# Half of w1's columns in blocks of 128, 128, 96 and 96 rows

## The chip, the core and the metric

The kernel runs on one core of one Trainium2 chip. The core has five engines with instruction streams of their own: PE (matrix multiplication), DVE (vector), ACT (activations), POOL and SP. 16 DMA engines move data between HBM and the on-chip memory; here only SP issues transfers. The metric is the device time of one execution in microseconds (us). Before the change the median of three runs is 676.2 us (675.98 to 676.47).

## The reference

A decode step for two rows of x (2 x 448): attention over a cache of 16 heads x 4096 positions x 256, and beside it a small two-layer network with a ReLU; a gate mixes the two. All in float32.

```python
q = (x @ wq).reshape(B, Sq, 16, 256).transpose(0, 2, 1, 3)
scores = jnp.einsum("bhqd,bhkd->bhqk", q, k_cache) * (256 ** -0.5)
o = jnp.einsum("bhqk,bhkd->bhqd", softmax(scores), v_cache)
a = o.transpose(0, 2, 1, 3).reshape(B, Sq, 4096) @ wo
b = jnp.maximum(x @ w1, 0) @ w2          # w1: 448 x 1792, w2: 1792 x 448
g = sigmoid((x * gate_w).sum(-1, keepdims=True))
return g * a + (1 - g) * b
```

## The kernel before

**Data.** Nearly all bytes are the cache: 32 units (2 rows x 16 heads), each 128 partitions x 64 KB, half K and half V (`kv`). The on-chip memory holds a ring of three slots of 64 KB per partition. Everything that is large goes through these slots: first `wq` and `xg` (slot 0), then the units in turn, at the end `w1` and `w2` (slot 0, as two parts of the array `wm`) and `wo` (slot 1). xg, the last columns of wq's rows, holds x and the gate's weights in chunks of the contraction.

**Order of the transfers.** SP issues all of them, so they form one queue, and each of the 16 DMA engines works off its own share in this order. SP waits until a slot is free (the semaphore `freed`, counted by DVE after each unit) and then issues the next load into it, so that one to two loads are always queued behind the running one. After the last unit come `w1` (L170), `w2` (L171) and, when unit 30 is done, six parts of `wo` (L175): 14, 8, 4, 3, 2 and 1 blocks of 448 columns, each with a semaphore of its own.

**The main loop.** For each unit PE multiplies q with K into `sc` (L131), DVE takes the maximum (L351), ACT the exponential (L318), and DVE multiplies V with it and sums, in eight instructions (L356). ACT keeps the result (L323).

**w1.** D = 448 is 3 x 128 + 64 (`KF` = 3 full chunks, `KC` = 4 chunks). The 1792 columns are four groups of 448 (`G` = 4, `FG` = 448); group g accumulates in the partitions 32 g to 32 g + 31 of `pa`. `project` (L108) does the full chunks with one matmul per chunk and group (L111). The last 64 rows of two groups are stacked in 128 partitions, and a stationary operand `xl` with zeros in the right places does both groups in one matmul of 64 columns (L114). So each half of w1's columns (two groups) has 6 x 448 + 448 columns in 128 partitions, and w1 has `W1` = 6272 columns in all. ACT makes `xr` (x repeated for the full chunks, L297), `xn` (L298) and `xl` (L301) from xg at the start.

**The tail on PE.** `pe_tail` waits for w1 (`w1_in`) and does chunks 0 and 1 (`hidden(0, 2)`), waits until all units are done (`freed` = 32), transposes the maxima `nm` and the sums `ls` of the partial softmaxes (L234, L235), does chunk 2, multiplies the weights `wb` of the parts (L238), and does the last chunk (`hidden(KF, KC)`). ACT then applies the ReLU (L327), PE transposes the result (L250, L252), ACT repeats it (L329, L332), and 14 matmuls with w2 follow (L258). DVE in the meantime scales the attention output and spreads it (`oc`, L372). Then wo: 26 blocks in `acc` as they land (L270), one copy (L375), a fold (L278), the last 6 blocks directly (L283), and the result goes out (L377, L178). A float32 matmul shows as two MATMUL records.

Of the kernel before, what the change touches and what calls it, by code (L numbers as in the profile page):

```python
# [4 lines left out]
AF = mybir.ActivationFunctionType  # L5
# [4 lines left out]
P, HP = 128, 64  # L10
G = 4
R = P // G
# [3 lines left out]
DIRECT = (3, 2, 1)  # L16


def gated_mix_decode(nc, wq, kv, wm, wo, out):
    U, _, SW = kv.shape  # L20
    D = 448
    B = 2
    RB = R // B
# [4 lines left out]
    KC, KF = 4, 3  # L28
    H = U // B
    HH = H // G  # L30
    NW = wq.shape[1] - KC * (B + 1)
    FG = 448
    NF = 14
    W1 = 2 * (2 * KF * FG + FG)
    DG = D // G
    NO = HH * J
    SCALE = float(DH) ** -0.5
    pe, dve, act, pool, sp = nc.tensor, nc.vector, nc.scalar, nc.gpsimd, nc.sync
# [12 lines left out]
    slot = [ring[:, i * SW:(i + 1) * SW] for i in range(SLOTS)]  # L51

    def sb(name, *shape):
        t = nc.alloc_sbuf_tensor(name, list(shape), F32)
        assert nc.sbuf_base <= first
        return t.ap()
# [6 lines left out]
    last_v, w1_in, w2_in = ev(), ev(), ev()  # L63
# [11 lines left out]
    xr = sb("xr", P, KF, P // B, B)  # L75
    xl = sb("xl", P, 2, RB, B)
    xn = sb("xn", P, P // B, B)
    ge = sb("ge", P, 1)
    gp = sb("gp", P, 1)
    omg = sb("omg", P, 1)  # L80
# [7 lines left out]
    p = sb("p", P, SG)  # L88
# [10 lines left out]
    pa = ps("pa", P, CW)  # L99
# [5 lines left out]
    def x_of(c, n=R):  # L105
        return xr[:, c].rearrange("p r b -> p (r b)")[:, :n]

    def project(dst, w, at, at_last, n, lo, hi):  # L108
        for c in range(lo, min(hi, KF)):
            for g in range(G):  # L110
                m = pe.matmul(dst[g * R:(g + 1) * R, :n], x_of(c), w[:, at(c, g):at(c, g) + n], start=(c == 0), stop=False)  # L111
        if hi == KC:
            for i in range(2):
                m = pe.matmul(dst[i * HP:(i + 1) * HP, :n], xl.rearrange("p j r b -> p (j r b)"),  # L114
                              w[:, at_last(i):at_last(i) + n], start=False, stop=True)
        return m

    xg = slot[0][:, NW:wq.shape[1]].rearrange("p (c b) -> p c b", c=KC)

    ident_0, ident_ok, par_ok, fold_ok, xl_0 = (ev() for _ in range(5))  # L120
    x_ok, gate_mm, gate_ok, ge_ok, gp_ok, omg_ok = (ev() for _ in range(6))
# [23 lines left out]
    ml_tr, nb_ok, e_ok, el_ok, rl_ok, wb_ok, wp_mm, os_ok, po_mm, oc_ok = (ev() for _ in range(10))  # L145
    acc_mm, a_ok, z_mm, res_ok = ev(), ev(), ev(), ev()
    w1 = slot[0][:, :W1]
    w2 = slot[0][:, W1:W1 + NF * D]
    w_o = slot[1]

    with nc.Block(no_gpsimd_drain=True) as block:

        @block.sync
        def _(_e):
            sp.wait_ge(q_mm, 2)
            sp.dma_start(slot[0], kv[2]).then_inc(slot_in[0], 16)
            with nc.Fori(0, LOOP - 2, engines=(ET.SP,)) as r:
                u0 = sp.snap(r * SLOTS)
                for k in range(SLOTS):
                    s = (k + 1) % SLOTS  # L160
                    sp.wait_ge(freed, u0 + k + 1)
                    sp.dma_start(slot[s], kv[bass.ds(u0 + k + SLOTS, 1)].rearrange("o p n -> (o p) n")  # L162
                                 ).then_inc(slot_in[s], 16)
            sp.wait_ge(freed, U - 4)
            sp.dma_start(slot[1], kv[U - 2]).then_inc(slot_in[1], 16)
            sp.wait_ge(freed, U - 3)
            sp.dma_start(slot[2][:, :SW // 2], kv[U - 1][:, :SW // 2]).then_inc(slot_in[2], 16)
            sp.dma_start(slot[2][:, SW // 2:], kv[U - 1][:, SW // 2:]).then_inc(last_v, 16)
            sp.wait_ge(freed, U - 2)
            sp.dma_start(w1, wm[:, :W1]).then_inc(w1_in, 16)  # L170
            sp.dma_start(w2, wm[:, W1:]).then_inc(w2_in, 16)  # L171
            sp.wait_ge(freed, U - 1)
            k = 0
            for n, s in zip(ACC + DIRECT, wo_in):
                sp.dma_start(w_o[:, k * D:(k + n) * D], wo[:, k * D:(k + n) * D]).then_inc(s, 16)  # L175
                k += n
            sp.wait_ge(res_ok, 1)
            sp.dma_start(out, res[0:7 * 15 + 1:7, :]).then_inc(out_sem, 16)  # L178
# [13 lines left out]
        def pe_main():  # L192
# [7 lines left out]
            for i in range(2):  # L200
                if i:
                    pe.wait_ge(q_ok, i)
                project(pb, slot[0][:, i * NW // 2:(i + 1) * NW // 2], lambda c, g: g * W + c * CW,
                        lambda i: G * W + i * CW, CW, 0, KC).then_inc(q_mm, 1)
# [18 lines left out]
                pe.end_ifs()  # L223

        def pe_tail():
            half = W1 // 2
            def hidden(lo, hi):
                return project(pa, w1, lambda c, g: g // 2 * half + (g % 2 * KF + c) * FG,
                               lambda i: i * half + 2 * KF * FG, FG, lo, hi)

            pe.wait_ge(w1_in, 16)
            hidden(0, 2)
            pe.wait_ge(freed, U)
            pe.transpose(pc[:U, :P], nm, ident)  # L234
            pe.transpose(pc[:U, P:2 * P], ls, ident).then_inc(ml_tr, 1)  # L235
            hidden(2, KF)
            pe.wait_ge(wb_ok, 1)
            pe.matmul(pb[:, :U], wb.rearrange("u g r -> u (g r)"), ident[:U, :U], start=True,  # L238
                      stop=True).then_inc(wp_mm, 1)
            hidden(KF, KC).then_inc(hid_mm, 1)  # L240
            pe.wait_ge(fold_ok, 1)
            pe.wait_ge(os_ok, 1)
            n = HH * B * J
            for g in range(G):
                m = pe.matmul(pc[g * R:(g + 1) * R, :n], sel,
                              os.rearrange("p u j -> p (u j)")[:, g * n:(g + 1) * n], start=True, stop=True)
            m.then_inc(po_mm, 1)
            pe.wait_ge(hid_ok, 1)
            for t in range(KF):
                pe.transpose(pb[:, t * P:(t + 1) * P], hs[:, t * P:(t + 1) * P], ident)  # L250
            for j in range(2):
                m = pe.matmul(pb[j * HP:(j + 1) * HP, KF * P:], hs[:, KF * P:], ident, start=True, stop=True)  # L252
            m.then_inc(hid_tr, 1)
            pe.wait_ge(w2_in, 16)
            pe.wait_ge(hr_ok, 1)
            for k in range(NF):
                g = k % G
                pe.matmul(acc[g * R:(g + 1) * R, :D], hr[:, k, :], w2[:, k * D:(k + 1) * D], start=(k < G),  # L258
                          stop=False)

            def o_of(k):
                return oc[:, k // J, k % J].rearrange("p r b -> p (r b)")

            pe.wait_ge(oc_ok, 1)
            k, n = 0, sum(ACC)
            for i, a in enumerate(ACC):
                pe.wait_ge(wo_in[i], 16)
                for _ in range(a):
                    g = k % G
                    m = pe.matmul(acc[g * R:(g + 1) * R, :D], o_of(k), w_o[:, k * D:(k + 1) * D], start=False,  # L270
                                  stop=(k >= n - G))
                    k += 1
            m.then_inc(acc_mm, 1)
            for i, a in enumerate(DIRECT):
                if i == 0:
                    pe.wait_ge(a_ok, 1)
                    for g in range(G):
                        pe.matmul(z[g * R:(g + 1) * R, :DG], fold.rearrange("p r b -> p (r b)"),  # L278
                                  a_sb[:, g * DG:(g + 1) * DG], start=(i == 0), stop=False)
                pe.wait_ge(wo_in[len(ACC) + i], 16)  # L280
                for _ in range(a):
                    for g in range(G):
                        m = pe.matmul(z[g * R:(g + 1) * R, :DG], o_of(k),  # L283
                                      w_o[:, k * D + g * DG:k * D + (g + 1) * DG], start=False,
                                      stop=(k == NO - 1))
                    k += 1
            m.then_inc(z_mm, 1)
# [7 lines left out]
        def _(_e):  # L295
            act.wait_ge(slot_in[0], 16)
            act.activation(xr, xg[:, :KF, None, :B].to_broadcast([P, KF, P // B, B]), AF.Copy)  # L297
            act.activation(xn, xg[:, KF:, :B].to_broadcast([P, P // B, B]), AF.Copy)  # L298
            act.wait_ge(xl_0, 1)
            for j in range(2):  # L300
                a = act.activation(xl[j * HP:(j + 1) * HP, j], xg[j * HP:(j + 1) * HP, KF:, :B]  # L301
                                   .to_broadcast([HP, RB, B]), AF.Copy)
            a.then_inc(x_ok, 1)
            act.wait_ge(gate_mm, 1)
# [1 line left out]
            for i in range(2):  # L306
# [3 lines left out]
                a = act.activation(qt[:, i * U // 2:(i + 1) * U // 2, :].rearrange("p (s n) t -> p s t n", s=2),  # L310
                                   pc.rearrange("p (s t x) -> p s t x", s=2, t=T)[:, :, :, ::17], AF.Copy)
# [18 lines left out]
            for j in range(2):  # L330
                r = slice(j * HP, (j + 1) * HP)
                a = act.activation(hr[r, KF * G:, :],  # L332
                                   pb[r, KF * P + j * HP:KF * P + (j + 1) * HP].rearrange("p (k r) -> p k r", r=R),
                                   AF.Copy)
# [103 lines left out]
```

## Time and profile before

| | us |
|---|---|
| median of 3 runs | 676.2 |
| the profiled execution | 676.38 |
| its span, first to last instruction | 674.8 |
| PE busy | 213.0 |
| DVE busy | 339.8 |
| ACT busy | 54.2 |

The profiled execution's own time is 1.6 us longer than its span; this is what lies before the first and after the last recorded instruction. A row of the timeline gives the start, the duration, the engine, the line and what the instruction writes and reads; in brackets stands the idle time before it and what ended it. A row of the table of windows gives for each engine the busy time and the number of instructions in that stretch, and then PE's granted clock, the mean busy share of the 16 DMA engines, and their rate. A row of the queue table gives the packets that started in the asked window, their megabytes, and the time that they took as a share of 16 engines over that window. Queue q1 holds the transfers that SP issues, q8 the loading of instructions.

### The profile page before, as it was taken

The page shows a single profiled execution, that of the slowest core. Times are in us where ns is not written, and L with a number is a line of the kernel's source. Part 1 is how long each engine was busy: PE and PEld are TensorE (multiplying, and loading weights), DVE is VectorE, ACT ScalarE, POOL GpSimd, SP SyncE. Part 2 cuts the span into 40 slices and gives each one's busy share as a digit, 9 for nine tenths or more (in the row PEclk, how much of TensorE's full clock was granted, in tenths as well). Part 3 has the DMA queues.
Part 4 walks back from the last instruction along what each step waited for, and adds up shares of the span by engine and source line. Part 5 has one row for each costly group of instructions (what it writes and reads, how often), then busy time and mean ns, then how long its engine had stood idle before and what let it go on. Part 6 is the DMA issues. An engine that isn't in the chain of part 4 may idle for free.

```text
span 674.8 us, 4173 instructions
## 1 busy us (share of the span) xinstructions
PE 213.0 (32%) x1279; PEld 52.0 (8%) x1279; DVE 339.8 (50%) x561; ACT 54.2 (8%) x144; POOL 1.1 (0%) x9
## 2 busy tenths in 40 slices
PE   0633221333332123333321233333222333332455
PEld 0210000000000000000000000000000000000011
DVE  0024566545455665544656654455566445456670
ACT  0110000000000000000000000000000000000110
POOL 0000000000000000000000000000000000000000
PEclk9976567767655676776656677665667767655879
DMA  9999999999999999999999999999999999999997
GB/s 381 427 435 436 435 435 435 435 435 435 435 435 435 435 435 435 435 435 435 431 435 435 435 435 435 435 435 435 435 435 435 435 435 435 435 435 406 420 437 304
DMA packets 6082, 289.59 MB, mean 429 GB/s; under 512 B 704, under 2 KB 832, under 8 KB 1216
## 3 DMA queue, kind: packets, MB, share of 16 engines
q1 hardware_dynamic: 6080, 289.55, 99.3%
q8 instruction: 2, 0.03, 0.0%
HBM read 289.54 MB, written 0.01 MB: 429 GB/s over the span
## 4 chain that ended last, share of the span: by engine, by line
DMA 70%; DVE 12%; PE 9%; issue 6%; DVEq 1%; ACT 1%; SPq 0%; ACTq 0%
DMA ring<-in_kv 65%; DVE ring L356 10%; PE sc L131 9%; DMA ring<-in_wo 4%; DVE nm L351 2%; DVEq L356 1%; ACT p L318 1%; PE z L283 0%; DVEq L348 0%; DVEq L353 0%; PE acc L270 0%; SPq L175 0%; SPq L162 0%; DVEq L351 0%; DVE a_sb L375 0%
## 5 line engine op out<-in xcount | busy, mean ns | idle before, releaser
L356 DVE SCALAR_TENSOR_TENSOR ring<-ring,p 128x1024 f32 x256 | 295.9, 1222 | 54.8 <-ACT p L318 54.8
L131 PE MATMUL sc<-ring,qc 128*32 128x512 f32 x1024 | 182.6, 878 | 417.8 <-DMA ring<-in_kv 417.8
L351 DVE TENSOR_REDUCE nm<-sc 128x1024 f32 x32 | 39.2, 1225 | 236.1 <-PE sc L131 236.1
L131 PEld LDWEIGHTS sc<-ring,qc 128*32 128x32 f32 x1024 | 41.2, 154 | 558.6 <-issue 558.6
L318 ACT ACTIVATE p<-sc,nm 128x1024 f32<-128x1024 f32 x32 | 35.7, 1114 | 257.8 <-DVE nm L351 257.8
L323 ACT ACTIVATE ov<-on 128x8 f32 x32 | 6.7, 208 | 309.0 <-DVE ring L356 309.0
L356 DVE DVE_READ_ACCUMULATOR ring<-ring,p 128x1 f32 x256 | 21.4, 83 | 0.0
L343 DVE TENSOR_SCALAR ge<-ge 128x1 f32<-128x1 f32 x1 | 0.2, 155 | 21.5 <-ACT ge L305 21.5
L196 PE MATMUL pa<-ring,xr 128*128 128x1 f32 x6 | 1.4, 356 | 21.4 <-ACT xl L301 21.4
L375 DVE COPY a_sb<-acc 128x448 f32<-128x448 f32 x1 | 0.6, 625 | 14.7 <-PE acc L270 14.7
L111 PE MATMUL pa<-ring,xr 128*32 128x448 f32 x24 | 4.2, 830 | 11.7 <-DMA ring<-in_wm 11.7
L270 PE MATMUL acc<-ring,oc 128*32 128x448 f32 x52 | 5.9, 544 | 4.7 <-DMA ring<-in_wo 4.7
L111 PE MATMUL pb<-ring,xr 128*32 128x512 f32 x48 | 7.1, 737 | 0.0
L318 ACT ACTIVATION_READ_ACCUMULATOR p<-sc,nm x32 | 6.2, 193 | 0.0
L320 ACT ACTIVATE qc<-qt x32 | 6.1, 192 | 0.0
L258 PE MATMUL acc<-ring,hr 128*32 128x448 f32 x28 | 3.2, 541 | 1.0 <-ACT hr L332 1.0
L196 PEld LDWEIGHTS pa<-ring,xr 128*128 128x128 f32 x6 | 1.4, 326 | 21.4 <-ACT xl L301 21.4
L270 PEld LDWEIGHTS acc<-ring,oc 128*32 128x32 f32 x52 | 1.7, 109 | 8.9 <-issue 5.9
L114 PE MATMUL pb<-ring,xl 128*64 128x512 f32 x8 | 2.2, 618 | 0.0
L297 ACT ACTIVATE xr<-ring 128x384 f32<-128x384 f32 x1 | 0.5, 522 | 18.3 <-DMA ring<-in_wq 18.3
L111 PEld LDWEIGHTS pb<-ring,xr 128*32 128x32 f32 x48 | 1.6, 132 | 3.9 <-issue 3.9
L308 ACT ACTIVATE q<-pb 128x512 f32<-128x512 f32 x2 | 1.2, 598 | 8.6 <-PE pb L114 8.6
(56 smaller groups left out, 23.7 us busy)
## 6 DMA issues: line engine op xcount, KB each, us to landing
ring<-in_kv SPq DMA_DIRECT2D x2, 4096.0 KB, 34.7
ring<-in_wq SPq DMA_DIRECT2D x1, 7174.0 KB, 19.5
ring<-in_wm SPq DMA_DIRECT2D x2, 3136.0 KB, 30.7
ring<-in_wo SPq DMA_DIRECT2D x1, 3136.0 KB, 24.4
ring<-in_wo SPq DMA_DIRECT2D x1, 1792.0 KB, 28.3
ring<-in_wo SPq DMA_DIRECT2D x1, 896.0 KB, 30.0
ring<-in_wo SPq DMA_DIRECT2D x1, 672.0 KB, 31.1
ring<-in_kv SPq DMA_DIRECT2D x31, 39.6
```

Of the source, the lines that this page charges most:

```text
L111: m = pe.matmul(dst[g * R:(g + 1) * R, :n], x_of(c), w[:, at(c, g):at(c, g) + n], start=(c == 0), stop=False)
L114: m = pe.matmul(dst[i * HP:(i + 1) * HP, :n], xl.rearrange("p j r b -> p (j r b)"), w[:, at_last(i):at_last(i) + n], start=False, stop=True)
L131: m = pe.matmul(sc[g * R:(g + 1) * R, c * CW:(c + 1) * CW], qc[:, s, t:t + 1].to_broadcast([P, R]), slot[s][:, lo:lo + CW], start=(t == 0) ...
L196: m = pe.matmul(pa[:, :1], x_of(c, P) if c < KF else xn[r].rearrange("p r b -> p (r b)"), xg[r, c, B:], start=(c == 0), stop=(c == KC - 1))
L258: pe.matmul(acc[g * R:(g + 1) * R, :D], hr[:, k, :], w2[:, k * D:(k + 1) * D], start=(k < G), stop=False)
L270: m = pe.matmul(acc[g * R:(g + 1) * R, :D], o_of(k), w_o[:, k * D:(k + 1) * D], start=False, stop=(k >= n - G))
L308: act.activation(q, pb, AF.Copy, scale=SCALE).then_inc(q_ok, 1)
L318: act.activation(p, sc, AF.Exp, bias=nm[:, bass.ds(u, 1)], accum_out=ls[:, bass.ds(u, 1)]).then_inc(raised, 1)
L320: act.activation(qf[:, bass.ds((u + 2) % SLOTS * T, T)], qt[:, bass.ds(u + 1, 1), :].rearrange("p o t -> p (o t)"), AF.Copy).then_inc(quer ...
L323: act.activation(ov[:, bass.ds(u, 1), :].rearrange("p o j -> p (o j)"), on, AF.Copy).then_inc(kept, 1)
L351: dve.tensor_reduce(nm[:, bass.ds(u, 1)], sc, axis=AX.X, op=ALU.max, negate=True).then_inc(maxed, 1)
L356: m = dve.scalar_tensor_tensor(v, v, 1.0, p, op0=ALU.mult, op1=ALU.mult, accum_out=on[:, j:j + 1])
```

## The change

One half of w1's columns (groups 0 and 1) stays as it was: three chunks of 128 rows and the stacked chunk of 64. The other half (groups 2 and 3) is contracted in blocks of 128, 128, 96 and 96 rows. Its two blocks of 128 lie in `w1` as before, behind the first half, and `W1` falls to 4928 columns. The two blocks of 96 lie in an array of their own, `we`, and are loaded by one more transfer into 96 partitions of slot 0 (`w1e`, 4 x 448 columns, 7168 B in each of 96 rows). `we` is an array of 12 x 9 rows of 11392 columns, of which the transfer reads rows 0 to 7 of every nine and the first 1792 columns. `wm` has 11392 columns: w1 is padded to 5120 (`AT`), and w2 follows; in the slot `w1e` starts at column 5120 and w2 at 6912. The semaphore `w1_in` is now raised by both transfers, and PE waits for 32 in place of 16.

x gets a fifth chunk in xg (96 rows for the second block of 96: the last 32 of chunk 2 and the last 64), so that each row of wq grows by three values, and ACT makes `xe` from it, ahead of xl. The first block of 96 uses the first 96 rows of xr's chunk 2. `hidden` is written out: chunks 0 and 1 as before, chunk 2 with 96 rows for groups 2 and 3, and a last chunk of three matmuls (one stacked for groups 0 and 1, one each for groups 2 and 3).

```diff
-    NW = wq.shape[1] - KC * (B + 1)
+    NW = wq.shape[1] - (KC + 1) * (B + 1)
-    W1 = 2 * (2 * KF * FG + FG)
+    PS = 96
+    W1 = 2 * KF * FG + FG + 4 * FG
+    WE = 4 * FG
+    AT = -(-W1 // 256) * 256
...
     w1 = slot[0][:, :W1]
-    w2 = slot[0][:, W1:W1 + NF * D]
+    w1e = slot[0][:PS, AT:AT + WE]
+    w2 = slot[0][:, AT + WE:AT + WE + NF * D]
...
             sp.dma_start(w1, wm[:, :W1]).then_inc(w1_in, 16)
-            sp.dma_start(w2, wm[:, W1:]).then_inc(w2_in, 16)
+            sp.dma_start(w1e, we[:, :8, :WE]).then_inc(w1_in, 16)
+            sp.dma_start(w2, wm[:, AT:]).then_inc(w2_in, 16)
...
-            half = W1 // 2
+            half = 2 * KF * FG + FG
+
             def hidden(lo, hi):
-                return project(pa, w1, lambda c, g: g // 2 * half + (g % 2 * KF + c) * FG,
-                               lambda i: i * half + 2 * KF * FG, FG, lo, hi)
-
-            pe.wait_ge(w1_in, 16)
+                for c in range(lo, hi):
+                    for g in range(G):
+                        i, h = divmod(g, 2)
+                        if i == 0 and c == KF:
+                            if g == 0:
+                                pe.matmul(pa[:HP, :FG], xl.rearrange("p j r b -> p (j r b)"),
+                                          w1[:, 2 * KF * FG:half], start=False, stop=True)
+                            continue
+                        x, at = x_of(c) if c < KF else xe.rearrange("p r b -> p (r b)"), (h * KF + c) * FG
+                        if i:
+                            at = half + (h * 2 + c) * FG if c < 2 else (h * 2 + c - 2) * FG
+                        w = w1e if i and c >= 2 else w1
+                        m = pe.matmul(pa[g * R:(g + 1) * R, :FG], x[:PS] if w is w1e else x, w[:, at:at + FG],
+                                      start=(c == 0), stop=(c == KC - 1))
+                return m
+
+            pe.wait_ge(w1_in, 32)
...
-            act.activation(xn, xg[:, KF:, :B].to_broadcast([P, P // B, B]), AF.Copy)
+            act.activation(xn, xg[:, KF:KC, :B].to_broadcast([P, P // B, B]), AF.Copy)
+            act.activation(xe, xg[:, KC:, :B].to_broadcast([P, RB, B]), AF.Copy)
...
+    we = np.zeros((PS // 8, 9, 11392), np.float32)
+    we[:, :8, :rest.shape[2]] = rest
+    w1 = np.concatenate([full, last, both], 1)
+    w1 = np.pad(w1, ((0, 0), (0, -w1.shape[1] % 256)))
```

More of the change, by code (lines that the diff above doesn't have):

```diff
@@ L16, with gated_mix_decode @@
 DIRECT = (3, 2, 1)
-def gated_mix_decode(nc, wq, kv, wm, wo, out):
+def gated_mix_decode(nc, wq, kv, wm, we, wo, out):
     U, _, SW = kv.shape
@@ L77, in gated_mix_decode @@
     xn = sb("xn", P, P // B, B)
+    xe = sb("xe", P, RB, B)
     ge = sb("ge", P, 1)
@@ L116, in project @@
         return m
-    xg = slot[0][:, NW:wq.shape[1]].rearrange("p (c b) -> p c b", c=KC)
+    xg = slot[0][:, NW:wq.shape[1]].rearrange("p (c b) -> p c b", c=KC + 1)
     ident_0, ident_ok, par_ok, fold_ok, xl_0 = (ev() for _ in range(5))
@@ L297, in _ @@
             act.activation(xr, xg[:, :KF, None, :B].to_broadcast([P, KF, P // B, B]), AF.Copy)
-            act.activation(xn, xg[:, KF:, :B].to_broadcast([P, P // B, B]), AF.Copy)
+            act.activation(xn, xg[:, KF:KC, :B].to_broadcast([P, P // B, B]), AF.Copy)
+            act.activation(xe, xg[:, KC:, :B].to_broadcast([P, RB, B]), AF.Copy)
             act.wait_ge(xl_0, 1)
             for j in range(2):
-                a = act.activation(xl[j * HP:(j + 1) * HP, j], xg[j * HP:(j + 1) * HP, KF:, :B]
+                a = act.activation(xl[j * HP:(j + 1) * HP, j], xg[j * HP:(j + 1) * HP, KF:KC, :B]
                                    .to_broadcast([HP, RB, B]), AF.Copy)
@@ L404 @@
     full, last = blocks(np.concatenate([np.asarray(A_x).reshape(B, D).T, np.asarray(gate_w).reshape(D, 1)], 1))
-    xg = np.concatenate([full, np.concatenate([last, last])[:, None]], 1)
+    PS = 96
+    ext = np.zeros((P, 1, B + 1), np.float32)
+    ext[:PS, 0] = np.concatenate([full[PS:, KF - 1], last])
+    xg = np.concatenate([full, np.concatenate([last, last])[:, None], ext], 1)
     kt = np.asarray(A_k_cache)[:, heads].reshape(B, H, S, T, P).transpose(1, 0, 4, 3, 2).reshape(U, P, T * S)
@@ L416 @@
     wo = np.asarray(A_wo).reshape(HH, G, R, J, D).transpose(1, 2, 0, 3, 4).reshape(P, -1)
-    full, last = blocks(B_w1)
-    full = full.reshape(P, KF, 2, 2, FG).transpose(0, 2, 3, 1, 4).reshape(P, 2, -1)
-    last = last.reshape(HP, 2, 2, FG).transpose(2, 0, 1, 3).reshape(P, 2, FG)
-    w1 = np.concatenate([full, last], 2).reshape(P, -1)
+    w1 = np.asarray(B_w1).reshape(D, 2, 2, FG)
+    full, last = blocks(w1[:, 0])
+    full = full.reshape(P, KF, 2, FG).transpose(0, 2, 1, 3).reshape(P, -1)
+    last = last.reshape(HP, 2, FG).transpose(1, 0, 2).reshape(P, FG)
+    both = w1[:2 * P, 1].reshape(2, P, 2, FG).transpose(1, 2, 0, 3).reshape(P, -1)
+    rest = w1[2 * P:, 1].reshape(2, PS, 2, FG).transpose(1, 2, 0, 3).reshape(PS // 8, 8, -1)
+    we = np.zeros((PS // 8, 9, 11392), np.float32)
+    we[:, :8, :rest.shape[2]] = rest
+    w1 = np.concatenate([full, last, both], 1)
+    w1 = np.pad(w1, ((0, 0), (0, -w1.shape[1] % 256)))
     w2 = np.asarray(B_w2).reshape(G, FG, D)
@@ L424 @@
     w2 = np.concatenate([full, last], 1).reshape(P, -1)
-    arrays = {"wq": wq, "kv": kv, "wm": np.concatenate([w1, w2], 1), "wo": wo}
+    arrays = {"wq": wq, "kv": kv, "wm": np.concatenate([w1, w2], 1), "we": we, "wo": wo}
     arrays = {n: np.ascontiguousarray(a) for n, a in arrays.items()}
```

## The prediction

> **What bounds the kernel now.** I read the page first: DMA share and rate in 40 slices, the DMA queues, and the engines' shares of the chain that ended last.
>
> ```profile
> DMA  9999999999999999999999999999999999999997
> GB/s 381 427 435 436 435 435 435 435 435 435 435 435 435 435 435 435 435 435 435 431 435 435 435 435 435 435 435 435 435 435 435 435 435 435 435 435 406 420 437 304
> ...
> q1 hardware_dynamic: 6080, 289.55, 99.3%
> q8 instruction: 2, 0.03, 0.0%
> ...
> DMA 70%; DVE 12%; PE 9%; issue 6%; DVEq 1%; ACT 1%; SPq 0%; ACTq 0%
> ```
>
> The 16 DMA engines are busy for 99.3% of the span and move 435 GB/s, 27.2 GB/s each, in nearly every slice. The bytes set the time, and the change keeps them: w1 is 448 x 1792 x 4 B = 3136 KB before, and 2464 KB + 672 KB after. What can change is how evenly these bytes lie on the engines, above all at the end. Next I read the last pieces of the chain in order of time (start, duration, work):
>
> ```profile
> 638.18 0.33 SPq L175
> 638.55 0.43 SPq L175
> 639.02 29.95 DMA ring<-in_wo
> 669.02 1.00 PE acc L270 x8
> 670.05 0.64 DVE a_sb L375
> 670.73 0.40 PE z L278 x8
> 671.12 1.53 PE z L283 x48
> 672.68 0.27 DVE res L377
> ```
>
> The chain waits for wo until 668.97 and then computes almost without a break; wo's last parts land under L283. A DMA that lands later moves all of this by its own delay. Third, the tail in windows (the last three columns: granted clock, DMA share, GB/s):
>
> ```profile
> 669.50:670.00 0.50, 0.48 (x8) 0.00 (x0) 0.00 (x0) 0.00 (x0) 0.00 (x0) 1.00 0.97 380
> 670.00:670.50 0.50, 0.00 (x0) 0.00 (x0) 0.45 (x1) 0.00 (x0) 0.00 (x0) 1.00 0.64 244
> 670.50:671.00 0.50, 0.27 (x12) 0.28 (x16) 0.17 (x1) 0.00 (x0) 0.00 (x0) 1.00 0.11 43
> 671.00:671.50 0.50, 0.50 (x32) 0.46 (x20) 0.00 (x0) 0.00 (x0) 0.00 (x0) 1.00 0.12 47
> 671.50:672.00 0.50, 0.50 (x23) 0.32 (x16) 0.00 (x0) 0.00 (x0) 0.00 (x0) 1.00 0.05 18
> ```
>
> A share of 0.11 or 0.12 is two engines of sixteen; 0.05 is one for most of the window. So 14 engines are done by about 670.5, one laggard, A, at about 671.4, and the last, B, at about 671.9. Where do the laggards come from? The queue table of short windows tells: first the q8 row of 62.7 to 63.5 us, then the q1 row of 65.15 to 65.85, then the packets of 65.85 to 67.5, then the q8 row of 659.80 to 659.83.
>
> ```profile
> q8 instruction: 1, 0.02, 7.5%
> ```
> ```profile
> q1 hardware_dynamic: 15, 0.98, 324.0%
> ```
> ```profile
> DMA packets 1, 0.07 MB, mean 40 GB/s; under 512 B 0, under 2 KB 0, under 8 KB 0
> ```
> ```profile
> q8 instruction: 1, 0.02, 200.0%
> ```
>
> At 63 us one engine carries a packet of instructions. In the next round of 64 KB packets 15 engines start within 0.7 us and the sixteenth only after that. While its queue is full, an engine can't make such a lag good. The second instruction packet comes at 659.8, some 11 us before the end. I read A and B as the engines that carried these two packets; nothing in the trace says which of the sixteen they are.
>
> **The change, part by part.** First, how the load is dealt out. One round of w2 packets (651.15 to 652.1):
>
> ```profile
> q1 hardware_dynamic: 16, 0.40, 98.0%
> ```
>
> Sixteen packets of 25.1 KB are sixteen rows of w2 (6272 columns x 4 B), one for each engine; 128 rows are thus 8 rows per engine. The new transfer has 96 rows of 7168 B, and its source is written as 12 groups of 8 rows, with a ninth row skipped after each, so that the groups can't be joined. Two ends bound the dealing. By groups, 12 engines take 8 rows, 57,344 B or 2.11 us at 27.2 GB/s, and four take none. Evenly, each takes 6 rows, 1.58 us, as these 672 KB cost now. I take 12 x 8, as the rows show 8 whole rows per engine. Then 12 engines end 2.11 - 1.58 = 0.53 us later than now and four end 1.58 us earlier. Each loaded engine also handles 16 packets for w1 in place of 8. Their price lies between nothing (rows of 64 KB and 25 KB both run near 435 GB/s) and 15 ns each (the last windows, with packets of 1.8 to 5.4 KB, still reach 380 GB/s: 2.7 KB in 114 ns in place of 99), so 0 to 0.12 us; I take 0.05, nearer to the large rows. Together +0.58.
>
> [...]
>
> The end then depends on where A and B sit. If B is among the loaded twelve, the last landing moves by +0.58. If only A is, A ends at 671.4 + 0.6 = 672.0 where B ended at 671.9: +0.1. If both are relieved, the twelve end at 670.5 + 0.6 = 671.1: -0.8, and the landing at 668.97 moves alike. If nothing is known, B is loaded in 12 cases of 16. I take **+0.58**.
>
> Second, the compute around it. Start and tail, from the timeline (start, us, engine, line; idle before in brackets):
>
> ```profile
> 20.71 0.29 ACT L298 ACTIVATE xn<-ring 128x128 f32<-128x128 f32 x1
> 20.91 0.45 ACT L301 ACTIVATE xl<-ring 64x32 f32<-64x32 f32 x2
> ...
> 33.76 0.33 SPq L156 DMA_DIRECT2D ring<-in_kv  x1
> ```
> ```profile
> 1.19 38.41 DMA ring<-in_kv
> 39.59 0.13 issue
> 39.72 5.57 PE sc L131 x32
> ```
> ```profile
> 619.99 0.33 SPq L170 DMA_DIRECT2D ring<-in_wm  x1
> 620.36 0.43 SPq L171 DMA_DIRECT2D ring<-in_wm  x1
> ```
> ```profile
> 647.26 3.21 PE L111 MATMUL pa<-ring,xr 128*32 128x448 f32 x16 [11.73 <-DMA ring<-in_wm]
> ...
> 650.40 0.40 PE L234 MATMUL pc<-ident,nm 128*32 128x128 f32 x1
> ...
> 652.62 0.97 PE L114 MATMUL pa<-ring,xl 128*64 128x448 f32 x4
> ...
> 653.91 1.42 DVE L372 COPY oc<-pc 128x256 f32<-128x256 f32 x4 [0.76 <-PE pc L245]
> ...
> 656.25 3.20 PE L258 MATMUL acc<-ring,hr 128*32 128x448 f32 x28 [1.01 <-ACT hr L332]
> ...
> 662.72 3.20 PE L270 MATMUL acc<-ring,oc 128*32 128x448 f32 x28 [3.27 <-DMA ring<-in_wo]
> ```
>
> The added ACT copy of xe is of the size of xl's or xn's, 0.2 to 0.3 us, ahead of the gate's matmul. It delays the load of kv[2] that SP issues at 33.76 to some 34.1; but the queue then still holds kv[0], which lands at 39.59, and kv[1] behind it, so 0. The 12 B that each row of wq grows by are 1.5 KB, 0.004 us. The extra issue on SP costs about 0.4 us at 620.4 while queued kv rows keep the engines busy, and w2 queued behind it is wanted 36 us later: 0. The wait on w1 now covers both transfers, and everything later on PE stands behind it, the transposes of nm and ls at 650.40 too. If it ends 0.6 later, at 647.8, the 16 matmul records (two for each matmul) end at 651.1 and the tail slides by up to 0.65. The last block has three matmuls in place of two; they lie in different columns of the array, so between 0 and 0.49 more (half of the 0.97), and ACT's ReLU waits for them; I take 0.2. The cover for all of it is PE's idle 3.27 us ahead of L270. DVE's chain to oc, which slides with the transposes, ends at 655.33, 7 us before L270 uses it. If that cover were gone, each microsecond would count whole.
>
> Sum against the profiled execution (676.38 us, of which the span is 674.8): 676.38 + 0.58 = 676.96. The median shown is 676.2, 0.18 below it: **676.8**.
>
> **The rivals.**
> - *Both laggards relieved:* -0.8, 675.4. For it: a relieved engine gains 1.58 us, more than A's lag of 0.9 and B's of 1.4. Against it: by counting alone, 1 case in 20; but instruction traffic could well stick to neighbouring engines, which the trace doesn't tell, so I give it more.
> - *No visible move:* even dealing, or only A loaded: 0 to +0.1, 676.2 to 676.3. The change would then not relieve any engine that matters.
> [...]
>
> [...]
>
> **How the numbers follow.** 0.2% is 1.35 us, about what a measurement of this kernel can tell from no change. Chances: forecast 0.33; no visible move 0.20; both relieved 0.20; ports 0.24, of which about 0.19 end above 677.55; something else 0.03. The first three all lie within 0.2%. So faster 0.03, same 0.77, slower 0.20. The range reaches from both relieved, with the spread of 0.2 of the times shown, 675.2, to the far end of the port rival, 678.9.
>
> **What would show it.** In the changed profile q1 has some 108 packets more (96 rows, 12 end marks) and the same 289.55 MB. If 12 engines are loaded and four relieved, the DMA share falls to about 0.75 from 669.0 on, as the four run out 2.1 us before the twelve; if the dealing is even, it stays near 1 until 670. Forecast right: the landing ahead of L270 x8 comes at about 669.5, and a share of 0.05 (B alone) lasts until 672.5. Both relieved: nothing is left after 671.2. [...] The covered steps are right if PE still idles some 3 us ahead of the first L270 group. The forecast is wrong if the second instruction packet vanishes or falls on another engine, as PE's program is one matmul longer: without B's lag the end would come 0.5 earlier.

## The result and the profile after

| | before | after |
|---|---|---|
| median, us | 676.18 | 679.64 |
| single executions, us | 675.98 to 676.47 | 678.10, 679.29, 680.43, 680.00 |
| the profiled execution, us | 676.38 | 678.10 |
| its span, us | 674.8 | 675.8 |

After to before is 1.0046, with a 95% interval of 1.0031 to 1.0060: slower, with medians 3.5 us apart, above the forecast (676.8) and above its range (675.2 to 678.9). Only 1.0 us of it shows in the span of the profiled execution; the three others have spans of 677.5, 677.8 and 678.7. So two things are to be explained: what the trace of after shows, and why most executions are worse than the traced one.

The page of after, DMA share and rate in 40 slices, queues and the chain's shares:

```profile
DMA  9999999999999999999999999999999999999997
GB/s 381 427 434 435 434 434 434 434 434 434 434 434 434 434 434 434 434 434 434 434 434 434 434 434 434 434 434 434 434 434 434 434 434 434 434 434 433 422 385 322
...
q1 hardware_dynamic: 6188, 289.56, 99.4%
q8 instruction: 2, 0.03, 0.0%
...
DMA 68%; DVE 12%; PE 11%; issue 6%; DVEq 1%; ACT 1%; SPq 0%; ACTq 0%
```

The bytes are the same, and q1 has 108 packets more: 96 rows and 12 end marks. But the last slice but one moves 385 GB/s in place of 437, at a busy share that still reads 9: the engines are busy without moving. Windows of 1 us show the place (after the window: busy time of PE, PEld, DVE, ACT, POOL, then granted clock, DMA share, GB/s):

```profile
643.00:644.00 1.00, 0.00 (x0) 0.00 (x0) 1.00 (x3) 0.00 (x0) 0.00 (x0) 0.50 1.04 394
644.00:645.00 1.00, 0.00 (x0) 0.00 (x0) 1.00 (x3) 0.00 (x0) 0.00 (x0) 0.50 0.97 228
645.00:646.00 1.00, 0.00 (x0) 0.00 (x0) 1.00 (x3) 0.00 (x0) 0.00 (x0) 0.50 1.14 265
646.00:647.00 1.00, 0.00 (x0) 0.00 (x0) 1.00 (x3) 0.00 (x0) 0.00 (x0) 0.50 0.82 179
647.00:648.00 1.00, 0.00 (x0) 0.00 (x0) 1.00 (x3) 0.00 (x0) 0.00 (x0) 0.50 1.43 391
```

From 644 to 647, while the 96 rows load (643.6 to 648.1), the rate is 179 to 265 GB/s at a share of 0.82 to 1.14. It isn't four idle engines: those are at w2 by then, and the share stays near 1. The timeline of PE shows what slides (start, us, what; in brackets the idle time before):

```profile
649.01 3.21 PE L247 MATMUL pa<-ring,xr 128*32 128x448 f32 x16 [14.17 <-DMA ring<-in_we]
652.16 0.40 PE L254 MATMUL pc<-ident,nm 128*32 128x128 f32 x1
...
658.88 3.20 PE L278 MATMUL acc<-ring,hr 128*32 128x448 f32 x28 [1.01 <-ACT hr L353]
663.66 3.20 PE L290 MATMUL acc<-ring,oc 128*32 128x448 f32 x28 [1.58 <-DMA ring<-in_wo]
```

w1's wait ends at 649.01 (before 647.26: +1.75), w2's matmuls start 2.63 later, and wo's first part 0.94 later. So the idle time ahead of wo, the cover of the whole computation, shrinks from 3.27 to 1.58 us. And the end of the chain in order of time:

```profile
639.86 30.04 DMA ring<-in_wo
669.94 1.00 PE acc L290 x8
672.05 1.55 PE z L303 x48
```

The landing comes at 669.90 (before 668.97), and the rest follows it as before. In this execution the transfers still set the end, 0.9 to 1.0 us late.

### The profile page after: what moved, and what is told of

Its sections match the earlier page's. It is cut to its first block, busy times and chain, and to the rows that moved or that the text cites. A ratio compares the mean times of both kernels' runs of the same rounds, so it can differ in the third digit from the quotient of the medians.

```text
span 675.8 us, 4179 instructions
## 1 busy us (share of the span) xinstructions
PE 214.2 (32%) x1281; PEld 52.2 (8%) x1281; DVE 339.8 (50%) x561; ACT 54.3 (8%) x145; POOL 1.1 (0%) x9
## 4 chain that ended last, share of the span: by engine, by line
DMA 68%; DVE 12%; PE 11%; issue 6%; DVEq 1%; ACT 1%; SPq 0%; ACTq 0%
DMA ring<-in_kv 64%; PE sc L135 10%; DVE ring L377 10%; DMA ring<-in_wo 4%; DVE nm L372 2%; DVEq L377 1%; ACT p L339 1%; PE z L303 0%; DVEq L369 0%; DVEq L374 0%; PE acc L290 0%; SPq L181 0%; SPq L167 0%; DVEq L372 0%; DVE a_sb L396 0%
## 5 line engine op out<-in xcount | busy, mean ns | idle before, releaser
L247 PE MATMUL pa<-ring,xr 128*32 128x448 f32 (+1 forms) x24 | 4.3, 847 | 14.2 <-DMA ring<-in_we 14.2
L393 DVE COPY oc<-pc 128x256 f32<-128x256 f32 x4 | 1.4, 418 | 1.5 <-PE pc L265 1.5
```

Of the source, the lines that this page charges most:

```text
L247: m = pe.matmul(pa[g * R:(g + 1) * R, :FG], x[:PS] if w is w1e else x, w[:, at:at + FG], start=(c == 0), stop=(c == KC - 1))
```

## The experiments

Times are medians in us; "before" is the kernel before, timed among the same executions. Spans are told where groups of executions matter, since they lack the 1.3 to 3.2 us outside the first and last instruction.

| kernel | median (range) | to before, 95% |
|---|---|---|
| plain (before, unaltered, one execution) | 676.96 | |
| again (after, unaltered) | 679.88 (677.74 to 680.14) | 1.0051 (1.0039 to 1.0063) |
| pair64 | 677.51 (677.14 to 680.52) | 1.0033 (1.0019 to 1.0047) |
| own64 | 676.38 (675.44 to 678.02) | 1.0005 (0.9996 to 1.0014) |
| even | 677.94 (677.53 to 678.98) | 1.0029 (1.0017 to 1.0041) |
| cut1 | 680.01 (677.96 to 681.28) | 1.0053 (1.0036 to 1.0070) |
| more1 | 676.16 (675.79 to 677.45) | 0.9998 (0.9990 to 1.0007) |
| own64cut | 677.29 (675.40 to 679.29) | 1.0009 (0.9995 to 1.0023) |
| warm_after | 679.48 (677.53 to 681.60) | 1.0050 (1.0036 to 1.0064) |
| warm_own64 | 676.98 (675.43 to 677.91) | 1.0004 (0.9995 to 1.0013) |
| warm_before | 676.33 (675.71 to 677.36) | 0.9996 (0.9987 to 1.0005) |
| sol | 676.36 (675.35 to 677.40) | 0.9995 (0.9986 to 1.0003) |
| light_after | 678.92 (676.96 to 680.81) | 1.0031 (1.0017 to 1.0044) |
| light_own64 | 675.22 (675.06 to 676.89) | 0.9991 (0.9982 to 0.9999) |
| light_before | 675.93 (675.67 to 676.58) | 0.9994 (0.9986 to 1.0003) |
| light_even | 678.13 (677.29 to 679.05) | 1.0023 (1.0014 to 1.0032) |
| light_drain | 681.64 (680.25 to 681.98) | 1.0073 (1.0059 to 1.0086) |

### Is it the way the rows are dealt?

`again` is the changed kernel once more. `pair64` and `own64` load only 64 rows of the two blocks, and differ in nothing but the way these rows are dealt: eight groups of eight rows, or, in two transfers of 32 rows, twice eight groups of four. `even` takes the skipped rows out of the array, so that all 16 engines carry six of the 96 rows each.

```diff
 # pair64
-            sp.dma_start(w1e, we[:, :8, :WE]).then_inc(w1_in, 16)
+            sp.dma_start(w1e, we[:8, :8, :WE]).then_inc(w1_in, 16)
 # own64
+            sp.dma_start(w1e[:R], we[:8, :4, :WE]).then_inc(w1_in, 16)
+            sp.dma_start(w1e[R:], we[8:16, :4, :WE]).then_inc(w1_in, 16)
 # even
+            sp.dma_start(w1e, we[:, :WE]).then_inc(w1_in, 16)
```

> The changed kernel once more, unaltered. Three theories of what slows all 16 engines to half while the 96 rows are loaded. [...] Layout: the reads of the new array, with its skipped ninth rows, are slow. Count: dealing to 12 engines is itself the loss. All three expect the DMA rate to fall to 180 to 265 GB/s for some 3 us before the w1 wait ends, as in the first trace, and a time near 679.6. The first trace's span was only 1.0 us above before's; if the other executions are longer for the same reason, the stretch of low rate is longer in them, 4 to 6 us; if not, the extra time lies elsewhere in the trace.

> Only 64 of the 96 rows are loaded and contracted (the last 32 rows of both blocks are left out), in 8 groups of 8, so that 8 engines carry 8 rows each. [...] Count: 8 engines at full pace, packets at 0.27 us, time 675.4 to 676.8.

> [...] Layout: slow as with pairs, 677.5 to 679.5. Count: as with pairs, 675.4 to 676.8.

> The 96 rows as one transfer without skipped rows, 6 rows for each of 16 engines (dealt evenly). [...] Layout: if the wide pitch is what hurts, as slow as the changed kernel, 678 to 680; if the skipped rows are, 676.2. Count: 676.2, no dip.

The windows of pair64, of own64 and of even, in this order:

```profile
644.00:645.00 1.00, 0.00 (x0) 0.00 (x0) 1.00 (x3) 0.00 (x0) 0.00 (x0) 0.50 0.77 203
645.00:646.00 1.00, 0.00 (x0) 0.00 (x0) 1.00 (x3) 0.00 (x0) 0.00 (x0) 0.50 1.37 315
646.00:647.00 1.00, 0.00 (x0) 0.00 (x0) 1.00 (x3) 0.00 (x0) 0.00 (x0) 0.50 0.84 190
```
```profile
644.00:645.00 1.00, 0.00 (x0) 0.00 (x0) 1.00 (x3) 0.00 (x0) 0.00 (x0) 0.50 0.97 410
645.00:646.00 1.00, 0.00 (x0) 0.00 (x0) 1.00 (x3) 0.00 (x0) 0.00 (x0) 0.50 1.14 487
646.00:647.00 1.00, 0.31 (x4) 0.20 (x8) 1.00 (x3) 0.00 (x0) 0.00 (x0) 0.50 1.18 509
```
```profile
645.00:646.00 1.00, 0.00 (x0) 0.00 (x0) 1.00 (x3) 0.00 (x0) 0.00 (x0) 0.50 0.98 244
646.00:647.00 1.00, 0.00 (x0) 0.00 (x0) 1.00 (x3) 0.00 (x0) 0.00 (x0) 0.50 1.64 484
647.00:648.00 1.00, 0.00 (x0) 0.00 (x0) 1.00 (x3) 0.00 (x0) 0.00 (x0) 0.50 0.97 340
648.00:649.00 1.00, 0.00 (x0) 0.00 (x0) 1.00 (x3) 0.00 (x0) 0.00 (x0) 0.50 0.79 308
```

With the same 64 rows and the same number of engines the rate falls to 190 to 315 GB/s in pair64 and stays at 410 to 509 in own64, where each of the 64 rows takes 0.27 us. In own64 w1's wait ends at 646.69 against 648.72 in pair64 and 649.01 in after. That settles that the dip comes from the way the rows are dealt, and not from the number of rows, engines or bytes, nor from the wide rows of the array, which own64 reads too. The six rows per engine of even bring a dip as well, to 244 GB/s, without skipped rows; its 677.94 lies above the 676.2 of Count and just below the 678 to 680 of a wide pitch.

Whether it is the partitions written at the same time or the rows read at the same time isn't shown: both change with the dealing (rows of the array that lie nine, five or six apart). Eight rows for each engine alone don't bring the dip: w1 and w2 of before, 128 rows high, run at 401 to 502 GB/s in windows of 1 us. And it isn't only some of the engines that lose: in after, 72 of the 96 rows took 0.42 to 0.56 us in place of 0.27, so at least nine of the twelve loaded engines had slow rows, and the first w2 packets on the four relieved ones took 1.5 to 1.7 in place of 0.93. No trace shows which engine writes what, and none shows a port; where the expectations name ports, the runs show this dip. Below, "collision" is short for it.

### Is it a longer program on TensorE?

The traces of `again` and `cut1` have a third instruction packet that meets the output. The waits on SP's queue, in after and in again (the three columns: total, times, longest):

```profile
SPq L404 <- DMA out<-res: 0.5, 1, 0.5
```
```profile
SPq L404 <- DMA out<-res: 1.6, 1, 1.6
```

The 1.1 us between them is the whole difference of the two spans (675.8, 676.9). Such a packet might come from the one matmul more. `cut1` is after without one of the last three matmuls (the last chunk of group 3 is left out), `more1` is before with `nm` transposed three times, and `own64cut` is own64 without one matmul.

```diff
 # cut1, own64cut
+                        if g == G - 1 and c == KF:
+                            continue
 # more1
+            pe.transpose(pc[:U, :P], nm, ident)
+            pe.transpose(pc[:U, :P], nm, ident)
```

> The changed kernel less one matmul: the contribution of the second block of 96 rows to the fourth group of columns is left out, so that PE's program is again as long as before's; all transfers stay. [...] Page: one matmul more carries PE's program over the end of a page of instructions, and a third packet of instructions is fetched near the end; where it falls on the output's transfer the end waits for it. Then without the matmul the third packet is gone, the executions lie close together, and only the ports are left: 677.3, all within 676.8 to 677.8. Load: the spread comes from the new transfer itself (its dip is longer in some executions): 679.6 as in the changed kernel, 677.7 to 680.4.

> The kernel before with PE's program made as much longer as in the change (the transpose of the maxima done three times, 0.8 us of work beside the waiting for wo); its transfers are untouched. Page: a third packet of instructions near the end, the times spread and the median 1 to 2.5 us above before, 677.3 to 678.8. Load: 676.3, no spread.

> [...] Page and ports together: no dip, no third packet, and both late engines relieved, so that the end comes 0.5 to 1.0 us before that of before: 675.3 to 675.8, close together. Load: spread as in the run with 64 rows, 675.4 to 678.0.

cut1 stays at 1.0053 and more1 at 0.9998: the theory fell. Third packets come in kernels with either number of instructions, and cost what the output happens to wait. The kernel before has one too in its second trace, `plain`, at 676.02, after the end of its span of 674.3; the two late engines of the tail are there again (last parts at 671.48 and 671.73, the other fourteen by 670.59). own64cut brought something else. No dip, all transfers landed at 671.2, and yet a span of 676.8 against own64's 673.8. Its timeline, and then its granted clock (the third column from the end):

```profile
651.29 3.35 PE L250 MATMUL pa<-ring,xr 128*32 128x448 f32 x8
...
661.77 4.82 PE L281 MATMUL acc<-ring,hr 128*32 128x448 f32 x26 [1.01 <-ACT hr L356]
...
666.46 5.77 PE L293 MATMUL acc<-ring,oc 128*32 128x448 f32 x50
```
```profile
654.00:658.00 4.00, 4.00 (x8) 0.96 (x6) 0.42 (x1) 0.00 (x0) 0.00 (x0) 0.50 0.99 426
658.00:662.00 4.00, 2.63 (x20) 1.22 (x23) 1.42 (x4) 1.45 (x4) 0.00 (x0) 0.50 0.98 422
662.00:666.00 4.00, 4.00 (x24) 1.10 (x18) 0.00 (x0) 0.00 (x0) 0.00 (x0) 0.52 1.00 419
```

The eight records of L250 take 3.35 us where own64's eight of L248 took 2.06, and from 661.77 on PE computes without waiting for wo: here PE sets the end, at a granted clock of 0.5 until 665.8. Own64's clock was at 1.0 from 651.4 to 658.2, at 0.5 until 661.6, and at 1.0 from there. A second theory for the changed kernel then: the collision eats the cover, and a slow clock in the tail does the rest.

### Is it TensorE's clock?

In after the granted clock was at 0.5 from 639.4 to 653.1. First I tried to keep it up with a loop of matmuls that nobody uses, from the release of unit 30 to w1's wait (10 passes in warm_after, 8 in warm_own64 and warm_before):

```diff
+            pe.wait_ge(freed, U - 1)
+            with nc.Fori(0, 10, engines=(ET.PE,)):
+                for g in range(G):
+                    pe.matmul(z[g * R:(g + 1) * R, :CW], x_of(0), q, start=True, stop=True)
             pe.wait_ge(w1_in, 32)
```

> The changed kernel with TensorE kept at work between the release of the last unit but one and the wait for w1: a loop of 10 passes over four matmuls of 512 columns (x's first block against q, into z, which is overwritten later), so some 40 matmuls of 0.12 us at full clock or 0.25 us at half. Nothing is left out. Ports alone (the last transfers land late and nothing else matters): 679.9 as without the loop, and the executions still scattered over 677.7 to 680.1. Ports and clock (the transfers land about 1 us late, and the rest of the loss is a TensorE that stays at a granted clock of 0.5 while it works off the tail): the granted clock is 1.0 ahead of 650, and the time is 677.3 (before's plus 1.0), with the executions within some 0.8 us. The dip of the rate between 643 and 649 stays in both.

> [...] Ports alone: 676.4 with executions from 675.4 to 678.0, as without the loop. Ports and clock: 675.4, the executions within some 0.6 us, since what scattered them was the clock.

> The kernel before with the same loop of 8 passes ahead of the wait for w1. Nothing is left out. Both theories: 676.2, no change, since its TensorE idles 3.27 us ahead of the last but three transfers and the transfers set the end. If it gets faster by more than 0.3 us, the clock costs the kernel before something too, and the 3.27 us of idle time were misread.

No time changed: warm_after stayed at 679.48, where 677.3 was expected if the clock had a part. But its windows say that this settles little:

```profile
650.00:654.00 4.00, 3.62 (x30) 1.03 (x24) 1.44 (x8) 0.46 (x2) 0.00 (x0) 1.00 0.99 426
654.00:658.00 4.00, 2.37 (x25) 1.04 (x23) 1.42 (x4) 1.44 (x4) 0.00 (x0) 0.96 0.93 401
658.00:662.00 4.00, 3.96 (x24) 1.23 (x16) 0.00 (x0) 0.00 (x0) 0.00 (x0) 0.61 1.07 457
```

The clock was at 1.0 until 657.7 (12 records of the loop took 1.50 us), and then at 0.5 until 661.1, after a stretch from 654 to 658 in which PE was busy for 2.37 of 4 us. So I took PE's time away instead: the tail's products on the upper 16 bits of each word; the lower half of the digits is left out. At a granted clock of 0.5 the first eight products of w1 then take 0.94 us (light_after) in place of 3.21 (after), 0.29 of it. light_own64 and light_before are own64 and before with the same products.

```diff
+        def hi(a):
+            return a.bitcast(mybir.dt.bfloat16)[:, 1::2]
-                pe.matmul(acc[g * R:(g + 1) * R, :D], hr[:, k, :], w2[:, k * D:(k + 1) * D], start=(k < G),
+                pe.matmul(acc[g * R:(g + 1) * R, :D], hi(hr[:, k, :]), hi(w2[:, k * D:(k + 1) * D]), start=(k < G),
```

> The changed kernel with the products of the tail (w1, w2 and wo) taken on the upper 16 bits of each word, read in place as bfloat16: the lower half of the digits is left out, transfers, order, waits and the number of instructions stay. TensorE then needs about a quarter of its time for a product of 448 columns, so that even at a granted clock of 0.5 it keeps ahead of wo. TensorE and its clock: 677.5 (the profiled executions' span of 675.8 and some 1.8 around it), the executions within about 1.2 us. Transfers: 679.7 as before, scattered over 677.5 to 680.5.

> [...] TensorE and its clock: 675.3, the executions within about 0.8 us. Transfers: 676.4 to 677.0 with executions from 675.4 to 678.

> The kernel before with the same lighter products. Its TensorE already waits 3.27 us for the last but three transfers, so both theories expect 676.0, at most 0.3 below before.

PE seems to have a part in the scatter: own64 falls from 676.38 to 675.22 (the intervals to before still touch), and its spans, 673.7 to 676.4 (own64cut's 673.6 to 678.0), become 673.4 to 675.2. But light_after misses its 677.5: 678.92, with spans from 675.3 to 679.2, though PE idles for 5.32 us ahead of wo in its trace. In the changed kernel most of the scatter isn't PE.

### Where does the late engine sit?

The trace of light_after is of one of the late executions, span 677.4. Its dip is that of after:

```profile
644.00:645.00 1.00, 0.00 (x0) 0.00 (x0) 1.00 (x3) 0.00 (x0) 0.00 (x0) 0.50 1.10 299
645.00:646.00 1.00, 0.00 (x0) 0.00 (x0) 1.00 (x3) 0.00 (x0) 0.00 (x0) 0.50 1.11 251
646.00:647.00 1.00, 0.00 (x0) 0.00 (x0) 1.00 (x3) 0.00 (x0) 0.00 (x0) 0.50 0.91 204
```

The end is not. After's last transfers first, then light_after's:

```profile
672.00:672.50 0.50, 0.50 (x28) 0.38 (x16) 0.00 (x0) 0.00 (x0) 0.00 (x0) 1.00 0.53 201
672.50:673.00 0.50, 0.50 (x24) 0.35 (x16) 0.00 (x0) 0.00 (x0) 0.00 (x0) 1.00 0.03 11
```
```profile
672.50:673.00 0.50, 0.08 (x4) 0.08 (x8) 0.37 (x1) 0.00 (x0) 0.00 (x0) 0.50 0.26 97
673.00:673.50 0.50, 0.50 (x18) 0.40 (x20) 0.00 (x0) 0.00 (x0) 0.00 (x0) 0.50 0.05 22
673.50:674.00 0.50, 0.30 (x16) 0.06 (x4) 0.00 (x0) 0.00 (x0) 0.00 (x0) 0.50 0.06 25
674.00:674.50 0.50, 0.21 (x8) 0.14 (x8) 0.00 (x0) 0.00 (x0) 0.00 (x0) 0.50 0.07 25
```

From 673.0 to 674.8 a share of 0.06 and 25 GB/s: one engine of sixteen, alone. PE waits for it, part by part:

```profile
674.29 0.38 PE L306 MATMUL z<-ring,oc 128*32 128x112 bf16 x8 [0.49 <-DMA ring<-in_wo]
674.89 0.28 PE L306 MATMUL z<-ring,oc 128*32 128x112 bf16 x4 [0.22 <-DMA ring<-in_wo]
```

Which one it is, the landings of the single engines tell, sorted by time (us of the span; twelve engines carry rows of the 96, sixteen carry wo):

```
              last unit, latest   w1, latest   96 rows                       wo's last part
after         639.44              646.50       648.00 ... 648.42 648.97      670.66 670.73 671.77 672.19 | 672.53 ... 673.12
light_after   639.55              646.52       648.19 ... 648.82 650.66      670.91 671.00 671.85 672.33 | 672.90 ... 673.24 674.84
```

In both, one engine has been about 0.9 us behind since the first instruction packet at 62.9 us: of each unit's sixteen landings from there on the last is 0.8 to 1.05 us behind the one before it. Its rows of w1 land at 646.5. In after it has none of the 96 rows: a loaded engine's land 4.0 us after its rows of w1, which would be 650.5, and all are in by 649.0. The time it saves hides its lag. In light_after its eight rows land at 650.66, 1.84 after the other eleven, and it ends 1.6 after everyone. The groups of executions fit that:

```
light_after (12 engines of 16 loaded)   675.3 675.5 675.5 675.8 | 677.2 677.4 677.4 677.8 | 678.7 679.2
light_own64 (8 engines of 16 loaded)    673.4 673.5 673.5 673.6 673.6 673.6 | 674.9 675.0 675.1 675.2 675.2
```

To test it, `light_even` gives all engines the same (the layout of even), and `light_drain` is to let the late engine catch up: SP waits once, before the last unit but one, until the unit ahead of it has landed.

```diff
 # light_drain
+            sp.wait_ge(slot_in[0], 16 * (U - 2) // 3 + 16)
             sp.wait_ge(freed, U - 4)
```

> The variant whose 96 rows stand without skipped rows, six for each of the 16 engines, with the tail's products on the upper 16 bits of each word (the lower half of the digits is left out). If the scatter is the place of the late engine: every engine carries the same, so one group of executions, spans of 675.9 to 676.5 (one with an instruction packet in the way of the output up to 1.2 more), time 677.7. If the collision itself varies: scattered over some 3 us like light_after, 675.3 to 679.2 of span.

> light_after with one wait more on the queue of SyncE: before it issues the last unit but one it waits until the last unit but two has landed, so that all engines start again together and the one that was late since 63 us no longer is. Nothing else changes; the wait costs the way of a transfer once, 2 to 3 us for all engines. If the scatter is the place of the late engine: the groups 675.5 and 677.4 fall together but for the second instruction packet at about 665 us (0.95 us on one engine, loaded or not), so that spans lie within about 1.3 us of each other, near 677.5 to 679. If the collision itself varies: a scatter of 3 to 4 us as before, near 677.5 to 681.5.

light_even has one group, spans of 675.7 to 677.4 with no gap above 0.4, where light_after spreads over 3.9 us; it spreads wider than expected, and its 678.13 lies above the 677.7. In light_drain's trace the wait does what it is for: the last unit's sixteen landings lie between 641.58 and 642.10, where light_after's latest, 639.55, is 0.9 behind the next. It costs about 3.3 us (641.58 in place of 638.33 for the first of them), more than expected (the 7 KB of the output took 1.7 us from issue to landing in before), and the five spans are 678.6, 679.1, 680.0, 680.3 and 680.3: 1.7 in place of 3.9, though two of the expected bounds (1.3, 679) are missed and five are few. Both speak for the place of the late engine and against a collision that varies by itself.

### A version without the collision

`sol` keeps before's blocks and only unstacks the last 64 rows of the second half: 64 rows of 896 columns, as two transfers of 32 rows in eight groups of four. Eight engines then carry 28,672 B more each (1.05 us at 27.2 GB/s), and eight carry as much less.

```diff
+            sp.dma_start(w1e[:R], we[:8, :4, :WE]).then_inc(w1_in, 16)
+            sp.dma_start(w1e[R:], we[8:16, :4, :WE]).then_inc(w1_in, 16)
```

> [...] Nothing is left out. Expected of the ports theory: no dip of the rate, the two late engines (A and B) are among the relieved eight, the loaded ones end at 670.5 + 1.05 = 671.5 instead of B's 671.9, so 675.8 (between 675.4 and 676.2). The clock theory adds that single executions can lie up to 2 us above that. If A or B were among the loaded engines: 677.2.

676.36, a ratio of 0.9995 (0.9986 to 1.0003): no change that can be told, and not the 675.8 expected. Its executions lie between 675.35 and 677.40; its traced one has no dip below 373 GB/s between 643 and 649. In that trace the last transfer lands at 671.47 (before 672.17), but PE computes from 660.20 to 670.46 without a wait for wo, at a granted clock of 0.5 from 653.6 to 663.9: what the transfers gain, PE takes away again.

## Why the prediction was wrong

- **The failed step:** "12 engines take 8 rows, 57,344 B or 2.11 us at 27.2 GB/s". The dealing was right (12 end marks, 12 landings), the rate was not. From the end of an engine's rows of w1 (643.9 to 644.4) to that of its rows of the 96 (648.0 to 648.4) it took about 4.0 us. The 0.24 given to ports, and the 678.9 at the end of the range, were estimates of mine; no run shows a port. What the runs put in the step's place is a rate that depends on how the rows are dealt: 0.27 us for each row in own64, 0.42 to 0.56 for most rows in after.
- **Why slower got only 0.20:** I took the 27.2 GB/s of the loads of 128 rows over to the 96 rows, as if these were dealt like those. No row of before showed which rows of a load of 128 each engine takes, so none could say what another dealing costs, and the groups of eight were there in the diff to be worked out.
- **The place of the laggards** was the right question, and the answer isn't one place. The traced execution has the late engine among the relieved (678.10, and in span +1.0), most others have it, by their spans, among the loaded (679.3 to 680.4, and in light_after +1.9 from group to group). The median of this change thus comes from the worse case.
- **"PE still idles some 3 us ahead of the first L270 group"** was wrong. w1's wait moved by 1.75, wo by 0.94, and the cover fell from 3.27 to 1.58. In the traced execution that was still enough. With PE's time taken away the ratio falls from 1.0051 (again) to 1.0031 (light_after), 1.3 us; the intervals overlap, so it isn't shown that PE has a part in after.
- **Right:** the bytes and their rate before the tail, 108 packets more, two instruction packets still there, no sign of the added ACT copy, SP issue or 12 B (the last unit's latest row lands at 639.44, before 639.75).
- **A small term mis-sized:** the third matmul in the last block was put at 0.2 us, at most 0.49. From the transposes to w2's first matmul PE takes 6.72 us in place of 5.85, and 6.70 in cut1, which has one matmul less. Before's two matmuls of the last block ran side by side from 652.62; in after xl's runs from 654.38 and xe's only from 655.27 on, and that makes the 0.87. It stayed under the cover.
- **The sum as it now stands, an estimate:** of 3.5 us, 1.0 is the collision with the late engine relieved (the span of after), up to 1.9 more the same with it loaded (the groups of light_after), and for the rest PE in the tail and an output that meets an instruction packet (1.1 in again) are candidates; that rest wasn't measured by itself.

Open stays what slows the rows. In light_after the late engine's last three rows still took 0.35, 0.48 and 0.60 us when the other eleven had finished theirs, so a second engine of the 96 isn't needed for a slow row. Open is also how the engine of the instruction packet is chosen. In the first, traced executions of after, again, cut1, warm_after, pair64 and the kernels of own64 it had no rows of w1e to load, while of 18 others of after, again, cut1 and warm_after only two have spans as low as 676.1. No late execution of the unaltered kernel was traced; that it is the same as in light_after is inferred from the spans. In light_after one relieved engine is also about 0.9 behind the other three, without a packet of instructions that would explain it; the cause is not known.

## What to carry to other kernels

When a transfer is cut to fewer rows, ask how its rows are dealt to the engines, and read what that costs from the rate in short windows at a full busy share: here 64 rows in groups of eight took the rate of all engines down to 190 to 315 GB/s (pair64), and in groups of four left it at 410 to 509 (own64). Here a queue that was full to the end carried a lag of 0.9 us of one engine from 62.9 us to the last unit, and with a load dealt unevenly the spans fell into groups 1.9 us apart (light_after); with one dealt evenly they had no gap above 0.4 (light_even). One trace of a kernel whose executions stand in groups shows one group only: look at the spans of all executions before you believe it.

## What was not expected of the hardware

- A badly dealt load holds up engines that carry none of it: at the dip all 16 together moved 179 to 265 GB/s, rows of the 96 took 0.42 to 0.56 us in place of 0.27, and w2's packets on the engines that had none of them 1.5 to 1.7 in place of 0.93.
- The granted clock of TensorE in the tail differs from execution to execution of nearly the same work: back at 1.0 at 651.4 in own64, only at 665.8 in own64cut, whose span is 3.0 us longer. A loop that held it at 1.0 up to 657.7 didn't keep it there: it fell to 0.5 until 661.1 in warm_after, as it did from 658.2 to 661.6 in own64, while in after it stayed at 1.0 from 653.1 to the end of the products.
- An instruction packet of 16 KB (0.94 us) just ahead of the 7 KB output cost 1.1 us of waiting in again.
